# Linear attention and two expert MLPs in one launch: another loading of the values and keys, and another order of the attention's operations

## The chip, the cores and the metric

The kernel runs on one core of one Trainium2 chip. The metric is the device time of one launch, in microseconds. Of the kernel before there are three timed runs, 710.43 to 712.17 us with a median of 711.64 us, and one profiled execution.

## The reference

Three stages follow one another; all numbers are float32.

```
phi(x) = [exp(p), exp(-p)],  p = x @ w_phi - max|x @ w_phi|     q, k: (2 batches, 8 heads, 576, 64); w_phi: (64, 128)
kv = phi(k)^T @ v,  z = sum over the sequence of phi(k)
attention = (phi(q) @ kv) / (phi(q) @ z + 1e-6)                  -> x: (1152, 512)
x = (x @ w_a) * (x @ w_b) @ w_out                                w_a, w_b: (512, 1536)
out = sum over 4 experts of p_e * (relu(x @ w1[e]) @ w2[e])      w1: (4, 512, 1024); p = normalised probabilities
```

## The kernel before

**The stages.** The attention comes first, then the first MLP, then the experts, with a little overlap at the borders. The MLPs' products are made in pairs of float32r parts (a high and a low part, three matmuls for one product), and their weights are prepared ahead of their use by ScalarE, VectorE and GpSimd while TensorE multiplies.

**The attention's keys.** Keys and queries come transposed, in chunks of six tiles of 128 columns (`load_chunk`, one tile buffer `xraw` each, XB = 3 of them). Tiles are taken in groups of four; the first group of keys has two. A group of keys goes through five steps, each known by one letter: `P` projects it with w_phi into PSUM (`pj`, L185), `x` takes the maximum off (VectorE, `mx` L200 and `r` L202, once for each half of the heads), `e` makes both exponentials (ScalarE, `kp`, L211 and L212), `k` multiplies one tile's features by the values and their ones into PSUM (`kv`, L235, 8 matmuls), and after a pair of heads has all its tiles `c` and `C` copy and add it to `kvz` (ScalarE L250, VectorE L254). A tile holds 128 positions of one pair of heads, or the last 64 positions of two pairs (a tile "m").

**The queries** go through `P` and `x` too, then `r` (transposes, `rt` L267), `E` (exponentials, `qp`), and `d`, `a`, `b` (`num` L302), with a denominator and a division on ScalarE and VectorE (`D`, `n`, `X`, `Y`).

**The values.** `load_v(b, st)` (L135) loads 128 positions of all heads of batch b by two DMAs, one for the six inner heads (L142) and one for the two outer ones (L146); the last 64 positions are loaded twice, to both halves of the partitions. A batch takes 12 DMAs. Of each 192 columns the middle 64 are ones, set by GpSimd (L132).

**What sets the order.** The string SCRIPT (L34) lists the steps letter by letter, and each engine gets its instructions in that order. `v` loads a part of batch 1's values, `w` runs one task of the weights' preparation, `f` one step of the first MLP's first unit, `p` normalises the probabilities. The weights' tasks come three to a piece of weight: `begin` (ScalarE, `m` L426 and `rn` L427, reads `raw`), `middle` (VectorE L434 to L440, GpSimd L443; at its end it issues the DMAs of the piece after next, 16 for two pieces of w_a and w_b), and `parts` (ScalarE L109, GpSimd L110). There are two `raw` buffers. All these loads are issued by SP, in program order; the first two pieces are asked for by `R`.

**A chunk that is loaded twice.** At set-up `load_chunk` is called for chunks 0 to 3. When chunk 0 is used up, `stage_proj` (L191) calls `load_chunk(0 + XB)`, chunk 3 once more, into another buffer. The first copy is never read. Chunk 4 is asked for when chunk 1 is used up, and so on.

**After the attention** the function `run` (L840) steps through units of matmuls, and after each step runs `tasks_per` tasks of the weights' preparation (1.9 in the first MLP's whole units, 1.8 in its blocks). `need(u)` runs at once what is still missing of a weight.

Of the kernel before, what the change touches and what calls it, by code (L numbers as in the profile page):

```python
# [9 lines left out]
F32 = mybir.dt.float32  # L10
# [6 lines left out]
B, H, S, D = 2, 8, 576, 64  # L17
# [8 lines left out]
NTB = NT // TB  # L26
HT = S // 2
WARM = 6
XB = 3
KB = 5  # L30
RB = 11
KQ = 3
LEAD = 2
SCRIPT = "PxPeVPRxexxkekexPxevkvekkvcxkexPCkexkkevckwxCvekkwPxxkwkckCePkkwxxkekkewcePCkwxxkkePqekcxCxPekkkwxceCxwekekPxkkxkwcCkPkkkxcxCPKrxrpExEPxrxwEEEEPxdrwDxnEPErwxwxEEaPrXbEExxXdPrYwDxExwanYEXPbYxrxwPErXEEdxEDxwYraEETnXwdwffwwDbYwaXnwwfYXbwYfffXwfY"  # L34
FP1 = FA // 2
FP2 = E * FE // 2

# [17 lines left out]
def tile_linear_attention_then_mlps(ctx, tc, qT, kT, v, w_phi, wab, wout, w12, probs, out):  # L55
# [40 lines left out]

    with tc.manual_schedule():
        nc.vector.memset(zero, 0.0)
        for h in range(2):
            nc.scalar.dma_start(out=ww[D * h:D * h + D], in_=w_phi)  # L100
        warm = duo("warm", (1,))
        for k in range(WARM):
            nc.tensor.matmul(out=warm[:, 0, 0:128], lhsT=zero, rhs=zero, start=True, stop=True)
# [11 lines left out]
        def load_chunk(n):  # L115


            if n >= 2 * B * 3:
                return
            t = r_p.tile([128, NC], F32, tag="xraw", name="xraw", bufs=XB)  # L120
            src = (kT if n < B * 3 else qT)[n % (B * 3)]
            step = 256 if n == 0 else NC
            for c in range(0, NC, step):
                nc.sync.dma_start(out=t[:, c:c + step], in_=src[:, c:c + step])
            xraw[n] = t

        vt = {}
        loaded = set()

        def alloc_v(b):  # L130
            t = k_p.tile([128, 5, NP, 192], F32, tag="v", name="v", bufs=2)
            nc.gpsimd.memset(t[:, :, :, 64:128], 1.0)  # L132
            vt[b] = t

        def load_v(b, st):  # L135

            loaded.add((b, st))
            rows = v[b, st * 128:min(S, (st + 1) * 128)]
            n = rows.shape[0]
            for lo in range(0, 128, n):  # L140
                o = vt[b][lo:lo + n, st].rearrange("p a c -> p (a c)")
                nc.sync.dma_start(  # L142
                    out=o[:, 128:128 + 3 * 192].rearrange("p (a c) -> p a c", c=192)[:, :, 0:128],
                    in_=rows[:, 1:H - 1, :].rearrange("s (a h) d -> s a (h d)", h=2),
                )
                nc.sync.dma_start(  # L146
                    out=o.rearrange("p (a c) -> p a c", c=64)[:, 0:4 * NP - NP:3 * NP - 1, :],
                    in_=rows[:, 0:H:H - 1, :],
                )

        def tiles_of_batch():
# [63 lines left out]
        def stage_kv(n, k):  # L215
            kp = st_kp[n]
            assert len(kp) == 2
            kind, b, t0, t = groups[n][k]
            t = seq[t]
            if t[0] == "m":  # L220
                parts = [(t[1], 4, 0, False, True), (t[2], 4, 1, True, False)]
            else:
                p, st = t
                first, last = st == 0, st == 3
                parts = [(p, st, 0, first, last and p % 2 == 1), (p, st, 1, first and p % 2 == 0, last)]
            for p, st, half, first, last in parts:
                assert (b, st) in loaded
                if (b, p) not in kv_ps:
                    kv_ps[b, p] = duo("kv", (2, 3))
            for h in range(2):  # L230
                for s in range(2):
                    for p, st, half, first, last in parts:
                        c = 256 * h + 128 * s
                        rows = slice(64 * half, 64 * half + 64)
                        nc.tensor.matmul(  # L235
                            out=kv_ps[b, p][:, half, c:c + 128],
                            lhsT=kp[h][rows, k, s, :],
                            rhs=vt[b][rows, st, p, 64 * h:64 * h + 128],
                            start=first and h + s == 0, stop=last, skip_group_check=True,
                        )  # L240
            if t[0] == "m":
                kv_done(b, t[1])
            elif t[1] == 3 and t[0] % 2 == 1:
                kv_done(b, t[0])
# [50 lines left out]
        def stage_num(qp, kvz, k):  # L295
            t = duo("num", (2, 3) if tail[0] else range(4))
            for i in range(2):
                for s in range(2):
                    for n in range(4):
                        h = n % 2  # L300
                        c = 64 * (1 - h) if k == 0 else 64 * h + 32 * (k - 1)
                        nc.tensor.matmul(  # L302
                            out=t[32 * n:32 * n + 32, i, 0:HT],
                            lhsT=kvz[n // 2][:, h, s, c:c + 32],
                            rhs=qp[n // 2][:, s, h, HT * i:HT * i + HT],
                            start=(s == 0), stop=(s == 1), tile_position=(0, 32 * n),
                        )
            return t
# [531 lines left out]
        def run(gen, rate, tasks_per):  # L840


            for _ in gen:
                tick()
                pos[0] += 1
                credit[0] = min(credit[0] + rate, 3.0)
                while credit[0] >= 1.0 and queue and queue[0][0] <= pos[0]:
                    queue.pop(0)[2]()
                    credit[0] -= 1.0
                credit[1] = min(credit[1] + tasks_per, 2.0)  # L850
                while credit[1] >= 1.0:
                    prep(1)
                    credit[1] -= 1.0


        load_chunk(0)
        alloc_v(0)
        load_chunk(1)
        load_v(0, 0)
        load_v(0, 1)  # L860
        load_chunk(2)
        for st in range(2, 5):
            load_v(0, st)
        load_chunk(3)

        def probabilities():
            nc.vector.tensor_reduce(out=psm, in_=pr, op=ALU.add, axis=AX.X)
# [55 lines left out]
        wait["P"] = [(n,) for n in range(NG)]  # L923
        wait["r"] = [(n,) for n in range(NKG, NG)]
        wait["d"] = [(b, half) for b in range(B) for half in range(2)]
        wait["v"] = [(1, st) for st in range(5)]
        acts = {
            "P": stage_proj, "x": stage_r, "e": stage_exp, "k": stage_kv, "c": kv_copy, "C": kv_add, "r": stage_rt,
            "E": stage_eq, "d": num, "D": num_den, "n": num_rc, "a": num_part, "b": num_part, "X": product_x,
# [21 lines left out]
        order += [(FP1 - 2, 0), (FP1 - 1, 0), (FP1 - 2, 1), None, (FP1 - 1, 1)]  # L951
        for jt in order:
            if jt is None:
                run(unit_h(0, 0), 1.2, 1.6)
                continue
            j, tp = jt
            if j in BLOCKS:
                run(block_ab(j, tp), 1.0, 1.8)
                continue
            if jt == (FP1 - 2, 0):  # L960
                xc[0] = m_p.tile([128, 2, 7, 2, HT], F32R, tag="xc", name="xc")
            run(unit_ab(j, tp) if j + tp else fill, 3.0 if j == FP1 - 1 else 2.0 if jt == (FP1 - 2, 1) else 1.0, 1.9)
        xt_p.release()
        w_p.release()
        l_p = ctx.enter_context(tc.tile_pool(name="l", bufs=1, side="left", reuse_waits="tile"))
# [5 lines left out]
        for j in range(FP2):  # L971
            for tp in range(2):
                if j + tp:

                    if j == 0:
                        credit[1] = 0.0
                    run(unit_h(j, tp), 0.3 if (j, tp) == (FP2 - 1, 1) else 0.7, 1 if j else 0.7)
        drain()


# [44 lines left out]
```

## Time and profile before

| | us |
|---|---|
| median of three timed runs | 711.64 (710.43 to 712.17) |
| the profiled execution: its own time | 712.72 |
| its span, first to last instruction | 710.8 |
| TensorE busy in the span | 697.3 |
| VectorE, ScalarE, GpSimd busy | 415.7, 297.1, 275.0 |

The profiled execution took 1.08 us more than the median, and 1.92 us of it lie outside its span. A busy time counts an instruction from start to end, also where it runs slowly or overlaps the next one. PE is TensorE's matmuls, PEld its weight loads, DVE VectorE, ACT ScalarE, POOL GpSimd, SP the sync engine that issues most DMAs. A float32 matmul leaves two records, so 16 records are 8 matmuls.

### The profile page before, as it was taken

To read this page: it belongs to the slowest core of one execution; us is meant where nothing else is said; L and a number is where in the kernel's file an instruction comes from. 1 tells how busy PE (TensorE), PEld (TensorE's weight loads), DVE (VectorE), ACT (ScalarE), POOL (GpSimd) and SP (SyncE) were. 2 spreads that over 40 slices of the span, in tenths; PEclk is the share of its full clock that TensorE was granted. 3 is DMA by queue.
4 is the path that set the end of the run, shared out by engine and by line. 5 is a ranking of instruction groups with operands and counts; after the bars stand their busy time and mean duration, and the time that the engine had idled before them with its cause. 6 is when DMAs were issued, how large, how long until landed. Compare 5 with 4: busy or idle time off the path is not lost.

```text
span 710.8 us, 13103 instructions
## 1 busy us (share of the span) xinstructions
PE 697.3 (98%) x5202; PEld 641.1 (90%) x5202; DVE 415.7 (58%) x721; ACT 297.1 (42%) x595; POOL 275.0 (39%) x241
## 2 busy tenths in 40 slices
PE   8988999999999999999999999999999999999998
PEld 8986679999999999999889888988888888888887
DVE  6769956666655565545455545554545454545454
ACT  5557845455444452323642433242324242424221
POOL 1212455454443456231663434443444344434200
PEclk9999999999999999999999999999999999999999
DMA  7643123232332330012221111211021101100003
GB/s 216 172 141 98 37 85 90 60 101 82 100 80 85 90 108 13 30 60 61 60 60 59 33 58 30 60 33 57 30 60 32 58 31 60 31 31 0 1 1 134
DMA packets 49854, 46.69 MB, mean 66 GB/s; under 512 B 8320, under 2 KB 41600, under 8 KB 49792
## 3 DMA queue, kind: packets, MB, share of 16 engines
q1 hardware_dynamic: 49488, 45.65, 22.0%
q8 instruction: 41, 0.67, 0.4%
q10 hardware_dynamic: 304, 0.20, 0.1%
q14 instruction: 21, 0.17, 0.1%
HBM read 43.47 MB, written 2.36 MB: 64 GB/s over the span
## 4 chain that ended last, share of the span: by engine, by line
PE 90%; DVE 3%; ACT 2%; DMA 2%; SPq 2%; issue 1%; ACTq 0%; DVEq 0%
PE acc L817 9%; PE acc L816 9%; PE acc L815 9%; PE X L598 5%; PE X L599 5%; PE X L600 5%; PE ab L682 5%; PE ab L684 4%; PE ab L683 4%; PE num L302 3%; PE acc L713 2%; PE acc L714 2%; PE Z L598 2%; PE Z L599 2%; PE acc L712 2%; PE Z L600 2%
## 5 line engine op out<-in xcount | busy, mean ns | idle before, releaser
L825 DVE SCALAR_TENSOR_TENSOR oacc<-acc,pr,oacc 128x512 f32<-128x512 f32 (+1 forms) x136 | 101.4, 746 | 116.3 <-PE acc L817 116.3
L110 POOL TENSOR_TENSOR w<-wx,w 128x512 fp32r<-128x512 f32 x68 | 89.5, 1319 | 158.0 <-ACT w L109 153.0
L817 PE MATMUL acc<-w,hhb 128*128 128x512 f32 x290 | 114.1, 394 | 0.0
L110 POOL TENSOR_TENSOR wc<-wt,wc 128x512 fp32r<-128x512 f32 (+1 forms) x48 | 70.7, 1501 | 111.1 <-ACT wc L109 107.0
L816 PE MATMUL acc<-w,hhb 128*128 128x512 f32 x290 | 113.5, 391 | 0.0
L815 PE MATMUL acc<-w,hhb 128*128 128x512 f32 x290 | 112.9, 389 | 0.0
L443 POOL TENSOR_TENSOR wx<-wx,rn 128x512 uint32<-128x512 uint32 x36 | 47.2, 1312 | 87.2 <-DVE wx L440 87.2
L598 PE MATMUL X<-xc,wc 128*128 128x288 f32 x256 | 77.1, 301 | 0.8 <-ACT h L603 0.8
L783 ACT ACTIVATE hhb<-h 128x288 fp32r<-128x288 f32 x64 | 36.2, 566 | 99.0 <-DVE h L606 99.0
L682 PE MATMUL ab<-xh,w 128*128 128x288 f32 x256 | 75.8, 296 | 0.0
L599 PE MATMUL X<-xc,wc 128*128 128x288 f32 x256 | 75.8, 296 | 0.0
L600 PE MATMUL X<-xc,wc 128*128 128x288 f32 x256 | 75.4, 295 | 0.0
L684 PE MATMUL ab<-xh,w 128*128 128x288 f32 x256 | 75.4, 294 | 0.0
L683 PE MATMUL ab<-xl,w 128*128 128x288 f32 x256 | 75.4, 294 | 0.0
L603 ACT ACTIVATE h<-X 128x288 f32<-128x288 f32 x64 | 26.0, 407 | 107.5 <-PE X L600 107.5
L817 PEld LDWEIGHTS acc<-w,hhb 128*128 128x128 f32 x290 | 54.5, 188 | 14.1 <-DVE hhb L784 2.8
L784 DVE SCALAR_TENSOR_TENSOR hhb<-h,hhb 128x288 fp32r<-128x288 f32 x64 | 40.9, 639 | 42.8 <-ACT hhb L783 42.8
L816 PEld LDWEIGHTS acc<-w,hhb 128*128 128x128 f32 x290 | 54.4, 188 | 8.3
L815 PEld LDWEIGHTS acc<-w,hhb 128*128 128x128 f32 x290 | 54.5, 188 | 7.8
L606 DVE TENSOR_TENSOR part<-acc,part 128x288 f32<-128x288 f32 (+2 forms) x80 | 34.5, 451 | 32.7 <-PE acc L770 18.2
L109 ACT ACTIVATE w<-wx 128x512 fp32r<-128x512 f32 x68 | 42.5, 628 | 24.1 <-POOL wx L443 18.7
L598 PEld LDWEIGHTS X<-xc,wc 128*128 128x128 f32 x256 | 48.0, 188 | 4.5 <-ACT h L603 1.3
(104 smaller groups left out, 1642.5 us busy)
## 6 DMA issues: line engine op xcount, KB each, us to landing
raw<-in_wab SPq DMA_DIRECT2D x192, 64.0 KB, 2.1
wt<-in_w SPq DMA_DIRECT2D x64, 128.0 KB, 2.4
wx<-in_w SPq DMA_DIRECT2D x32, 256.0 KB, 3.0
raw<-in_wout SPq DMA_DIRECT2D x12, 512.0 KB, 3.6
xraw<-in_kT SPq DMA_DIRECT2D x6, 384.0 KB, 4.5
xraw<-in_qT SPq DMA_DIRECT2D x6, 384.0 KB, 3.1
out<-oacc SPq DMA_DIRECT2D x8, 256.0 KB, 2.0
v<-in_v SPq DMA_DIRECT2D x8, 192.0 KB, 5.1
```

The source lines that it names most:

```text
L110: eng.tensor_tensor(out=lo, in0=src, in1=hi.bitcast(F32), op=ALU.subtract)
L443: nc.gpsimd.tensor_tensor(out=x, in0=x, in1=r, op=ALU.add)
L598: nc.tensor.matmul(out=ps, lhsT=whi, rhs=xhi, start=first and a == 0, stop=False, skip_group_check=True)
L599: nc.tensor.matmul(out=ps, lhsT=whi, rhs=xlo, start=False, stop=False, skip_group_check=True)
L600: nc.tensor.matmul(out=ps, lhsT=wlo, rhs=xhi, start=False, stop=a == 1, skip_group_check=True)
L682: nc.tensor.matmul(out=t, lhsT=whi, rhs=hi, start=(c == 0), stop=False)
L683: nc.tensor.matmul(out=t, lhsT=whi, rhs=lo, start=False, stop=False)
L684: nc.tensor.matmul(out=t, lhsT=wlo, rhs=hi, start=False, stop=(c == KD - 1))
L815: nc.tensor.matmul(out=acc, lhsT=hi, rhs=whi, start=f == 0, stop=False)
L816: nc.tensor.matmul(out=acc, lhsT=hi, rhs=wlo, start=False, stop=False)
L817: nc.tensor.matmul(out=acc, lhsT=lo, rhs=whi, start=False, stop=f == 1)
L825: nc.vector.scalar_tensor_tensor(out=o, in0=acc, scalar=sc, in1=o, op0=ALU.mult, op1=ALU.add)
```

## The change

- **Values by pairs.** The 64 columns of ones now stand outside the 128 columns of a pair's two heads (13 blocks of 64 instead of 12). `load_v(b, p)` loads one pair of heads for the first 512 positions by one DMA; `load_v(b, "m")` loads the last 64 positions of all pairs by two. A batch takes 6 DMAs instead of 12, and the first pair's values are the first to be loaded. The columns that L235 and L302 read change with it.
- **Keys.** XB is 4 instead of 3, the second chunk comes in three pieces as the first does, and at set-up only chunks 0 to 3 are loaded, with chunk 4 asked for when chunk 0 is used up: each chunk is loaded once.
- **w_phi.** Its second copy is issued by GpSimd's queue instead of ScalarE's.
- **Order and sizes.** A new SCRIPT; KB (buffers of `kp`) 6 instead of 5, RB (of `r`) 8 instead of 11; other numbers of preparation tasks in a step (1.3 for 1.9, 1.6 for 1.8, 1.9 for 1.6, 0.4 for 0.7).

```diff
-XB = 3
-KB = 5
-RB = 11
+XB = 4
+KB = 6
+RB = 8
-SCRIPT = "PxPeVPRxexxkekexPxevkvekkvcxkexPCkexkkevckwxCvekkwPxxkwkckCePkkwxxkekkew...
+SCRIPT = "PPxxeRexkexekPkVkxxPkexxevkecPvkxvkkCvexewckPkxkCwevxkkckCwkkePPwewxekxk...
-        for h in range(2):
-            nc.scalar.dma_start(out=ww[D * h:D * h + D], in_=w_phi)
+        for h, eng in enumerate((nc.scalar, nc.gpsimd)):
+            eng.dma_start(out=ww[D * h:D * h + D], in_=w_phi)
-            step = 256 if n == 0 else NC
+            step = 256 if n < 2 else NC
+        VORDER = [0, "m", 1, 2, 3]
-            t = k_p.tile([128, 5, NP, 192], F32, tag="v", name="v", bufs=2)
-            nc.gpsimd.memset(t[:, :, :, 64:128], 1.0)
+            t = k_p.tile([128, 5, 64 * (3 * NP + 1)], F32, tag="v", name="v", bufs=2)
+            nc.gpsimd.memset(t.rearrange("p s (a c) -> p s a c", c=64)[:, :, 0:3 * NP + 1:3], 1.0)
-        def load_v(b, st):
-            loaded.add((b, st))
-            rows = v[b, st * 128:min(S, (st + 1) * 128)]
-            n = rows.shape[0]
-            for lo in range(0, 128, n):
-                o = vt[b][lo:lo + n, st].rearrange("p a c -> p (a c)")
+        def load_v(b, p):
+            loaded.add((b, p))
+            if p == "m":
+                for k in range(2):
+                    nc.sync.dma_start(
+                        out=vt[b][64 * k:64 * k + 64, 4, 64:].rearrange("s (a c) -> s a c", c=192)[:, k:NP:2, 0:128],
+                        in_=v[b, 512:S].rearrange("s (a h) d -> s a (h d)", h=2)[:, k:NP:2],
+                    )
+            else:
+                c = 192 * p + 64
                 nc.sync.dma_start(
-                    out=o[:, 128:128 + 3 * 192].rearrange("p (a c) -> p a c", c=192)[:, :, 0:128],
-                    in_=rows[:, 1:H - 1, :].rearrange("s (a h) d -> s a (h d)", h=2),
-                )
-                nc.sync.dma_start(
-                    out=o.rearrange("p (a c) -> p a c", c=64)[:, 0:4 * NP - NP:3 * NP - 1, :],
-                    in_=rows[:, 0:H:H - 1, :],
+                    out=vt[b][:, 0:4, c:c + 128],
+                    in_=v[b, 0:512, 2 * p:2 * p + 2, :].rearrange("(t s) h d -> s t (h d)", t=4),
                 )
-                            rhs=vt[b][rows, st, p, 64 * h:64 * h + 128],
+                            rhs=vt[b][rows, st, 192 * p + 128 * h:192 * p + 128 * h + 128],
-                        c = 64 * (1 - h) if k == 0 else 64 * h + 32 * (k - 1)
+                        c = 64 * h if k == 0 else 64 * (1 - h) + 32 * (k - 1)
         load_chunk(0)
         alloc_v(0)
+        load_v(0, 0)
         load_chunk(1)
-        load_v(0, 0)
+        load_v(0, "m")
         load_v(0, 1)
-        load_chunk(2)
-        for st in range(2, 5):
-            load_v(0, st)
-        load_chunk(3)
+        for n in range(2, XB):
+            load_chunk(n)
+            load_v(0, n)
-                run(unit_h(0, 0), 1.2, 1.6)
+                run(unit_h(0, 0), 1.2, 1.9)
-                run(block_ab(j, tp), 1.0, 1.8)
+                run(block_ab(j, tp), 1.0, 1.6)
-            run(unit_ab(j, tp) if j + tp else fill, 3.0 if j == FP1 - 1 else 2.0 if jt == (FP1 - 2, 1) else 1.0, 1.9)
+            run(unit_ab(j, tp) if j + tp else fill, 3.0 if j == FP1 - 1 else 2.0 if jt == (FP1 - 2, 1) else 1.0, 1.3)
-                    run(unit_h(j, tp), 0.3 if (j, tp) == (FP2 - 1, 1) else 0.7, 1 if j else 0.7)
+                    run(unit_h(j, tp), 0.3 if (j, tp) == (FP2 - 1, 1) else 0.7, 1 if j else 0.4)
```

The order of instructions follows from these. Line numbers behind L132 grow by one or two in the changed kernel.

SP's queue, in the kernel before, from the last chunk of keys but one to the third and fourth piece of `raw` (`raw<-in_wab`, 8 DMAs each); ahead of these rows stand the 16 DMAs of the first two pieces, a chunk, and six DMAs of batch 1's values:

```order
L124 DMA xraw<-in_kT 128x768
L142 DMA v<-in_v 128x3x128
L146 DMA v<-in_v 128x2x64
L142 DMA v<-in_v 64x3x128
L146 DMA v<-in_v 64x2x64
L142 DMA v<-in_v 64x3x128
L146 DMA v<-in_v 64x2x64
L404 DMA raw<-in_wab 32x2x256 x8
L124 DMA xraw<-in_qT 128x768
L404 DMA raw<-in_wab 32x2x256 x8
```
The same queue in the changed kernel, from chunk 4 and the 16 DMAs of the first two pieces on:

```order
L124 DMA xraw<-in_kT 128x768
L406 DMA raw<-in_wab 32x2x256 x16
L124 DMA xraw<-in_kT 128x768
L148 DMA v<-in_v 128x4x128
L124 DMA xraw<-in_qT 128x768
L142 DMA v<-in_v 64x2x128 x2
L148 DMA v<-in_v 128x4x128 x2
L406 DMA raw<-in_wab 32x2x256 x8
L148 DMA v<-in_v 128x4x128
L124 DMA xraw<-in_qT 128x768 x2
L406 DMA raw<-in_wab 32x2x256 x8
```
Between the 16 DMAs of the first two pieces and the third piece stood 14 DMAs (two chunks and all 12 of batch 1's values); now it is 7 (two chunks and five of the values).

ScalarE, in the kernel before, around the third `begin` (the rows `m` and `rn`); `kp` are exponentials of keys, `kvz` a finished pair of heads, `w` a piece of weight:

```order
L211 ACTIVATE kp<-r 128x4x128
L212 ACTIVATE kp<-r 128x4x128
L250 COPY kvz<-kv 128x512
L211 ACTIVATE kp<-r 128x4x128
L212 ACTIVATE kp<-r 128x4x128
L426 ACTIVATE m<-raw 128x512
L427 ACTIVATE rn<-raw 128x512
L211 ACTIVATE kp<-r 128x4x128
L212 ACTIVATE kp<-r 128x4x128
L211 ACTIVATE kp<-r 128x4x128
L212 ACTIVATE kp<-r 128x4x128
```
The same place in the changed kernel:

```order
L213 ACTIVATE kp<-r 128x4x128
L214 ACTIVATE kp<-r 128x4x128
L252 COPY kvz<-kv 128x512
L213 ACTIVATE kp<-r 128x4x128
L214 ACTIVATE kp<-r 128x4x128
L428 ACTIVATE m<-raw 128x512
L429 ACTIVATE rn<-raw 128x512
L252 COPY kvz<-kv 128x512
L109 ACTIVATE w<-wx 128x512
L213 ACTIVATE kp<-r 128x4x128
L214 ACTIVATE kp<-r 128x4x128
```
The third `begin` has the same place in ScalarE's order, and behind it a pair's copy and the `parts` of a piece of weight come ahead of the next exponentials.

TensorE at the start, before (`warm` are six matmuls of zeros, `pj` projections, `kv` keys by values):

```order
L103 MATMUL warm<-zero 128x128 x6
L185 MATMUL pj<-ww,xraw 128x128 x20
L235 MATMUL kv<-v,kp 128x128 x16
L185 MATMUL pj<-ww,xraw 128x128 x8
L235 MATMUL kv<-v,kp 128x128 x32
L185 MATMUL pj<-ww,xraw 128x128 x8
L235 MATMUL kv<-v,kp 128x128 x48
L185 MATMUL pj<-ww,xraw 128x128 x8
```
And in the changed kernel:

```order
L103 MATMUL warm<-zero 128x128 x6
L187 MATMUL pj<-ww,xraw 128x128 x12
L237 MATMUL kv<-v,kp 128x128 x16
L187 MATMUL pj<-ww,xraw 128x128 x8
L237 MATMUL kv<-v,kp 128x128 x16
L187 MATMUL pj<-ww,xraw 128x128 x8
L237 MATMUL kv<-v,kp 128x128 x16
L187 MATMUL pj<-ww,xraw 128x128 x8
L237 MATMUL kv<-v,kp 128x128 x32
L187 MATMUL pj<-ww,xraw 128x128 x8
```
The third group's projection (the first of the single `x8` rows) moves behind the first group's two tiles, and the fourth group's stands behind 32 matmuls of `kv` instead of 16. The fifth stands behind 48 in both.

## Rows read from the trace of the kernel before

**Rows 1.** The page's first lines: span, and each engine's busy time.
```profile
span 710.8 us, 13103 instructions
...
PE 697.3 (98%) x5202; PEld 641.1 (90%) x5202; DVE 415.7 (58%) x721; ACT 297.1 (42%) x595; POOL 275.0 (39%) x241
```

**Rows 2.** Stretches: us; busy PE, PEld, DVE, ACT, POOL; PEclk, DMA share, GB/s.
```profile
4.00:24.50 20.50, 19.73 (x326) 19.44 (x328) 16.88 (x29) 12.96 (x25) 1.27 (x1) 1.00 0.72 199
24.50:38.70 14.20, 13.51 (x238) 13.12 (x234) 9.96 (x16) 6.97 (x14) 2.55 (x2) 1.00 0.74 207
38.70:47.30 8.60, 6.36 (x64) 5.59 (x66) 4.91 (x11) 7.24 (x15) 1.27 (x1) 0.80 0.55 154
...
55.00:70.00 15.00, 11.46 (x208) 8.37 (x206) 14.12 (x28) 12.44 (x30) 3.82 (x3) 1.00 0.37 115
70.00:90.00 20.00, 19.84 (x336) 12.21 (x332) 18.87 (x33) 16.32 (x36) 9.40 (x7) 1.00 0.17 42
...
105.00:707.40 602.40, 600.45 (x3736) 560.46 (x3735) 335.54 (x581) 229.90 (x458) 244.52 (x213) 1.00 0.19 55
```

**Rows 3.** The stretch with the lower clock, cut finer (columns as above).
```profile
38.70:42.90 4.20, 1.97 (x16) 1.20 (x16) 0.73 (x2) 4.20 (x9) 0.00 (x0) 1.00 0.77 200
42.90:46.40 3.50, 3.49 (x34) 3.49 (x36) 3.40 (x8) 3.04 (x7) 1.27 (x1) 0.54 0.43 139
```

**Rows 4.** Timeline 31 to 47: start us, length us, work [idle before, releaser].
```profile
31.17 4.76 SPq L404 DMA_DIRECT2D raw<-in_wab  x8
...
38.38 0.66 ACT L426 ACTIVATE m<-raw 128x512 f32<-128x512 f32 x1 [7.23 <-DMA raw<-in_wab]
...
40.16 2.05 PE L235 MATMUL kv<-v,kp 64*128 64x128 f32 x16 [1.49 <-ACT kp L211]
...
42.17 0.69 DVE L254 TENSOR_TENSOR kvz<-kv,kvz 128x512 f32<-128x512 f32 x1 [5.16 <-ACT kvz L250]
...
42.91 3.55 PE L235 MATMUL kv<-v,kp 64*128 64x128 f32 x32 [0.71 <-DVE kvz L254]
```

**Rows 5.** Timeline of SP's queue, 11 to 31.
```profile
11.85 10.54 SPq L404 DMA_DIRECT2D raw<-in_wab  x16
...
22.43 0.42 SPq L124 DMA_DIRECT2D xraw<-in_kT  x1
...
30.44 0.62 SPq L146 DMA_DIRECT2D v<-in_v  x1
```

**Rows 6.** Timeline of TensorE's weight loads and matmuls, 15 to 26.
```profile
15.57 5.44 PEld L235 LDWEIGHTS kv<-v,kp 64*128 64x128 f32 x96
...
25.89 0.72 PE L185 MATMUL pj<-ww,xraw 64*128 64x128 f32 x8 [0.66 <-DMA xraw<-in_kT]
```

**Rows 7.** DMA issues of the whole run: KB each, median us to landing.
```profile
raw<-in_wab SPq DMA_DIRECT2D x192, 64.0 KB, 2.1
...
xraw<-in_kT SPq DMA_DIRECT2D x6, 384.0 KB, 4.5
...
v<-in_v SPq DMA_DIRECT2D x8, 192.0 KB, 5.1
...
ww<-in_w_phi ACTq DMA_DIRECT2D x2, 32.0 KB, 2.7
```

**Rows 8.** Timeline of the start: ACT's queue, TensorE, VectorE.
```profile
0.73 1.20 ACTq L100 DMA_DIRECT2D ww<-in_w_phi  x2
...
1.05 2.93 PE L103 MATMUL warm<-zero 128*128 128x128 f32 x12 [1.05 <-DVE psm L105]
...
7.29 1.16 PE L185 MATMUL pj<-ww,xraw 64*128 64x128 f32 x16 [0.77 <-PE pj L185]
...
9.75 0.68 DVE L200 TENSOR_REDUCE mx<-pj 128x4 f32<-128x512 f32 x1
```

**Rows 9.** What TensorE waited for, 105 to 711: us in total, times, longest.
```profile
PE X L598 <- ACT h L603: 0.8, 2, 0.5
```

**Rows 10.** Timeline of POOL, 270 to 400.
```profile
341.32 4.56 POOL L110 TENSOR_TENSOR wc<-wt,wc 128x768 fp32r<-128x768 f32 x3 [7.59 <-ACT wc L109]
```

More of the change, by code (lines that the diff above doesn't have):

```diff
@@ L28 @@
 WARM = 6
-XB = 3
-KB = 5
-RB = 11
+XB = 4
+KB = 6
+RB = 8
 KQ = 3
 LEAD = 2
-SCRIPT = "PxPeVPRxexxkekexPxevkvekkvcxkexPCkexkkevckwxCvekkwPxxkwkckCePkkwxxkekkewcePCkwxxkkePqekcxCxPekkkwxceCxwekekPxkkxkwcCkPkkkxcxCPKrxrpExEPxrxwEEEEPxdrwDxnEPErwxwxEEaPrXbEExxXdPrYwDxExwanYEXPbYxrxwPErXEEdxEDxwYraEETnXwdwffwwDbYwaXnwwfYXbwYfffXwfY"
+SCRIPT = "PPxxeRexkexekPkVkxxPkexxevkecPvkxvkkCvexewckPkxkCwevxkkckCwkkePPwewxekxkcCekkxxkkwcPwkkexexeqeCPxkkkPckewwkxCkkkxekPwkxkcpCxxcPCKxrPEErExxErPExxwrEEEdPxDwraxnxXPbrxwxEEEXPwrxdEYaDxEPnEXwbrYYEEPxwxXxrdExrEwDEYTnEawfwwXfdbwbawwDwwXYYwfnfffXXwfYY"
 FP1 = FA // 2
@@ L226, in stage_kv @@
             for p, st, half, first, last in parts:
-                assert (b, st) in loaded
+                assert (b, p if st < 4 else "m") in loaded
                 if (b, p) not in kv_ps:
@@ L925, in tile_linear_attention_then_mlps @@
         wait["d"] = [(b, half) for b in range(B) for half in range(2)]
-        wait["v"] = [(1, st) for st in range(5)]
+        wait["v"] = [(1, p) for p in VORDER]
         acts = {
```

## The prediction

> **What bounds the kernel now.** I read the page's first lines, then the busy times by stretch, then the waits and the timeline of the stretches in which TensorE is not full. TensorE is busy 697.3 of 710.8 us [rows 1]; a whole-run share of 98% says nothing of where the rest lies. By stretch it is this [rows 2]: from 105 to 707.4 TensorE works 600.45 of 602.40 us, so what comes before 105 only shifts that block, and it is worth little to look for time inside it. From 70 to 90 it works 19.84 of 20.00. From 55 to 70 it works 11.46 of 15.00 while VectorE works 14.12, so the queries' start is VectorE's. From 4 to 24.5 TensorE works 19.73 of 20.50. The gap is at 38.7 to 47.3: 6.36 busy of 8.60, at a granted clock of 0.80 instead of 1.00.
>
> The timeline of that gap [rows 4] shows a chain. SP issues the third piece of `raw` only at 31.17 (8 DMAs in 4.76 us). ScalarE reaches its third `begin` at 38.38 - 7.23 = 31.15 and stands until 38.38 for these data. Behind it in its queue are exponentials of keys and the copy of a finished pair; so TensorE waits 1.49 us for exponentials at 40.16, VectorE 5.16 us for the copy at 42.17, and TensorE 0.71 us more at 42.91. After that idling the clock is granted at 0.54 from 42.9 to 46.4 [rows 3], which is near the lower of its two levels (1.2 of 2.4 GHz). The rest is paid in slow matmuls: the 32 records at 42.91 take 3.55 us.
>
> The size of the loss: 96 records of `kv`, six tiles, take 5.44 us, 0.91 us a tile of 16 records [rows 6]; a projection of 16 records takes about as much (1.16 us with its drain [rows 8]). From 38.7 to 47.3 TensorE runs 64 records [rows 2], four such lots, 4 x 0.91 = 3.64 us. 8.60 - 3.64 = 4.96, so **5.0 us** are lost there.
>
> Why the third piece is late stands in SP's queue [rows 5]: 16 DMAs of pieces one and two from 11.85 to 22.4, then 14 DMAs (two chunks, twelve of values) from 22.43 to 31.06, then the third piece.
>
> **The change part by part.**
>
> *Values by pairs, keys once.* After the 16 DMAs SP has 7 to issue instead of 14. The 14 took 31.06 - 22.43 = 8.63 us, 0.62 each [rows 5], so 7 x 0.62 = 4.3 us go. Ahead of the 16 stood 19 DMAs that began at about 0.7 and ended at 11.85, 0.59 each; now there are 15 (two more for the second chunk's pieces, six fewer for the values; chunk 4 stands where chunk 3's second copy stood), 4 x 0.59 = 2.4 us. The third piece can be issued 4.3 + 2.4 = 6.7 us earlier: 31.17 - 6.7 = 24.5. With its own 4.76 us and 2.1 us to land [rows 7] it is there at 31.3, against 38.0 before. The third `begin` stands at the same place of ScalarE's order, behind equally many exponentials, copies and `begin`s, so ScalarE comes to it at about 31.2. Its wait falls from 7.23 us to about nothing. TensorE lost 5.0 us to a wait of 7.23, so some 2.2 us of such a wait are hidden by tiles whose exponentials are ready; a rest of up to 2.2 us costs nothing. Value: **-5.0**, bounds -5.0 and 0.
>
> Next late: the bytes. Up to the third piece there are 7 chunks x 384 KB, 4 x 256 + 2 x 64 KB of batch 0's values, 3 x 256 + 2 x 64 KB of batch 1's, and 3 pieces x 512 KB: 6272 KB, 6.4 MB. The trace moved 199 and 207 GB/s in the two early stretches [rows 2]: 31 to 32 us, plus the 0.7 us of the start. So the transfers themselves could hold the piece to 33, 1.8 us after ScalarE's 31.2, inside the 2.2 us. That is narrow, and a rival below.
>
> [...]
>
> *The chunk that came late.* At 25.89 TensorE waited 0.66 us for a chunk of keys [rows 6]; it is chunk 4, issued at 22.43 behind the 16 DMAs [rows 5]. It now stands ahead of them. Value **-0.7**, bounds -0.7 and 0.
>
> *The start.* The third group's projection ran at 7.29 after an idle 0.77 us, for 1.16 us, to 8.45, and VectorE took it up at 9.75, when it had done the second group [rows 8]. Now two tiles of `kv`, 2 x 0.91, stand ahead of it. If they fill the idle time from 6.5 on, it ends at 6.53 + 1.82 + 0.91 = 9.3 and VectorE loses nothing. If their exponentials come so late that they begin only where that projection ended, at 8.45, it ends at 8.45 + 1.82 + 0.91 = 11.2, 1.4 us late for VectorE. I take **+0.5**, nearer the first, because in the trace these tiles wait for nothing behind that projection, so their exponentials are there by 8.45 and may be there earlier. In the keys TensorE is nearly full, so a delay here is a delay of the end.
>
> *w_phi by two queues.* ScalarE issued both halves in 1.20 us from 0.73, and such a DMA lands in 2.7 us [rows 7, 8]: the second at 0.73 + 0.60 + 2.7 = 4.0, when the warming matmuls end (1.05 + 2.93 [rows 8]). A DMA from GpSimd is not in the trace. Issued at 0.73 like the first half it can land at 3.4, which gains nothing, since the warming matmuls stand ahead; if it lands as slowly as the values (5.1 us [rows 7], at 5.8), it costs 1.8. I take **0**, by the row of the same transfer.
>
> *Buffers and the ones.* In the new string at most five `r` are alive at once (counted letter by letter), so RB = 8 does not bind, and a sixth `kp` only loosens: 0. The wider setting of the ones is GpSimd's, which from 4 to 24.5 is busy 1.27 us [rows 2]: 0.
>
> *Fewer preparation tasks in a step.* The same tasks run, later. In before TensorE waited for no weight after 105: the longest sum in its list is 0.8 us for a copy of ScalarE's [rows 9]. Counting steps in the code, the last part of w_a and w_b's eleventh and twelfth pieces comes 3 and 2 steps ahead of its use instead of 6, and of the experts' second w1 0 instead of 2. Before, the fourth piece of w_a and w_b already stood only 1 step ahead, and no wait came of it. TensorE lacks 1.95 us of the 602.40 after 105 [rows 2], so no more than that can be won. Value 0, bounds -1.9 and +7.5 (below).
>
> *The queries' order.* The same instructions in VectorE's stretch 55 to 70; both ends taken from its TensorE idle time there, 3.54 us [rows 2]: half of it gained or lost, +-1.8. Value 0, since VectorE's 14.12 of 15.00 leave it little to gain.
>
> **Sum**: -5.0 - 0.7 + 0.5 = -5.2 us. The profiled execution took 712.72 us (710.8 span and 1.92 around it), so it would be 707.5; it stands 1.08 us above the median of the runs, so the median goes from 711.64 to **706.4**.
>
> **Rivals.**
>
> *The bytes hold the piece.* If the early transfers run at before's mean up to the third piece rather than at 200 GB/s (7 chunks, 2560 KB of values and 3 pieces are 6784 KB, 6.95 MB, in the 37.3 us to 38.0: 186 GB/s), 6.42 MB need 34.5 + 0.7 us, and ScalarE waits 4.0 us, 1.8 more than is hidden. For it: 0.72 of the DMA engines' time was already taken. Against it: SP's issuing, 0.6 us a DMA, explains before without it. -5.2 + 1.8 = -3.4: 708.2.
>
> *VectorE's stretch takes it back.* If the queries' new order makes VectorE wait as long as TensorE is now early, the change does not do what it shortens: 711.6. For it: VectorE is the bound there. Against: its work is the same, and its 5.16 us of idling at 42 goes.
>
> *Weights come late* (the slower side). One mechanism, at the weights with the short lead. `parts` of the experts' second w1 took GpSimd 341.32 to 345.88 [rows 10] with two steps in hand; a lag of the same chain by about 2.5 us at three places (eleventh and twelfth piece, second w1) is 7.5 us of waiting TensorE: -5.2 + 7.5 = +2.3: 713.9. It decides when the sum of TensorE's waits for weights after 105 passes 5 us. For it: the shorter leads. Against: the piece at lead 1 in before cost nothing.
>
> **How the numbers follow.** The forecast has 0.66, the bytes 0.13, VectorE 0.10, the weights 0.11. The likeliest alone reaches from 704.1 (no start cost, 0.5, and 1.8 of the queries' idle) to 708.5 (1.4 instead of 0.5 at the start, and 1.2 lost in the queries' order). The range that should hold 8 of 10 goes from 703.8 to 711.2: it takes in the bytes and leaves out VectorE's case, the slower one and a few hundredths below. About 0.3%, 2.1 us, is what can be told from no change: faster 0.66 + 0.11 of the bytes' = 0.77; within, 0.12; slower 0.11.
>
> **What would show it.** Right: ScalarE's wait at its third `begin` is under 2.2 us; no stretch before 55 has a granted clock below 0.9 after the start; the last keys' tiles end about 5 us earlier than before, and VectorE's full stretch begins as much earlier. Start: the third group's projection ends between 9.3 and 11.2. Wrong: a long ScalarE wait for `raw` at the third or fourth `begin`; TensorE waits behind a `w` after 105; VectorE idle over 2 us between 50 and 65.

## The result

The changed kernel takes **705.77 us**, median of six executions (705.35 to 706.11), against 711.90 (710.43 to 715.84) of the kernel before on the same chip: ratio **0.9901 (0.9874 to 0.9929)**. The forecast was 706.4. Its profiled execution has a span of 703.8 us, 7.0 less than before [rows 1]; why the span gained more than the median comes with the experiments.

The page's first lines, spans and busy times as before:

```profile
span 703.8 us, 13086 instructions
...
PE 694.3 (99%) x5202; PEld 638.3 (91%) x5202; DVE 413.2 (59%) x721; ACT 295.5 (42%) x595; POOL 274.5 (39%) x242
```

Busy time by stretch (us; busy PE, PEld, DVE, ACT, POOL; granted clock, DMA share, GB/s), the counterpart of [rows 2], with the stretch from 47.3 added and the last one cut at 700:

```profile
4.00:24.50 20.50, 19.90 (x336) 19.34 (x338) 17.27 (x29) 13.73 (x27) 2.21 (x2) 1.00 0.71 203
24.50:38.70 14.20, 14.14 (x246) 13.71 (x244) 12.62 (x23) 10.64 (x22) 4.08 (x4) 1.00 0.84 240
38.70:47.30 8.60, 8.60 (x159) 8.60 (x158) 7.63 (x15) 5.71 (x13) 2.55 (x2) 1.00 0.37 124
47.30:55.00 7.70, 5.74 (x117) 5.33 (x116) 7.49 (x14) 5.67 (x16) 0.00 (x0) 1.00 0.33 102
55.00:70.00 15.00, 14.11 (x242) 8.92 (x242) 14.41 (x27) 9.81 (x21) 3.82 (x4) 1.00 0.12 39
70.00:90.00 20.00, 19.76 (x296) 12.52 (x291) 18.12 (x29) 15.99 (x36) 12.00 (x11) 1.00 0.26 77
90.00:105.00 15.00, 15.00 (x145) 13.30 (x136) 8.71 (x14) 8.71 (x16) 9.42 (x7) 1.00 0.28 77
105.00:700.00 595.00, 593.74 (x3686) 553.73 (x3685) 326.05 (x574) 223.77 (x450) 237.52 (x209) 1.00 0.18 54
```

The gap is closed: from 38.7 to 47.3 TensorE runs 159 records, at full clock, where it ran 64. The new thin stretch is 47.3 to 55, the queries' start, where VectorE is the full engine (7.49 of 7.70). This stretch began about 55 before.

The clock from 42.9 to 46.4, 0.54 in [rows 3], is 1.00:

```profile
42.90:46.40 3.50, 3.50 (x68) 3.50 (x66) 3.36 (x7) 1.70 (x4) 1.27 (x1) 1.00 0.34 133
```

The timeline around the third `begin` (start us, length us, work, in brackets idle before and its releaser), the counterpart of [rows 4]:

```profile
27.01 4.84 SPq L406 DMA_DIRECT2D raw<-in_wab  x8
...
33.90 1.96 PE L237 MATMUL kv<-v,kp 64*128 64x128 f32 x32
...
33.95 0.67 ACT L428 ACTIVATE m<-raw 128x512 f32<-128x512 f32 x1 [2.80 <-DMA raw<-in_wab]
...
36.14 3.57 PE L237 MATMUL kv<-v,kp 64*128 64x128 f32 x48
...
40.43 5.53 PE L237 MATMUL kv<-v,kp 64*128 64x128 f32 x96
```

ScalarE still waits 2.80 us for the third piece, but TensorE has tiles all the while: it is busy 14.14 of 14.20 us and 8.60 of 8.60 us in the two stretches around the wait. The last keys: the first transposes of queries (`rt`), which follow the last keys' projection, began at 54.9 and now begin at 48.9; the first MLP's first product with `hhb` began at 112.6 and now begins at 106.0. So 6.0 of the 7.0 us are there when the queries' transposes begin, 6.6 at that product. Before and after, by tile and by line (duration ns least, median, most, then first and last start):

```profile
L267 PE MATMUL rt<-ident,r x144: 216/222/273, 54.9 to 85.8; 64*128 64x64 f32 x144
...
L712 PE MATMUL acc<-hhb,w x128: 288/294/397, 112.6 to 334.7; 128*128 128x288 f32 x128
```
```profile
L269 PE MATMUL rt<-ident,r x144: 216/223/274, 48.9 to 79.2; 64*128 64x64 f32 x144
...
L714 PE MATMUL acc<-hhb,w x128: 288/295/399, 106.0 to 327.6; 128*128 128x288 f32 x128
```

### The profile page after: what moved, and what is told of

Read it like the earlier page. It is cut to its first block, busy times and chain, and to the rows that moved or that the text cites. A ratio compares the mean times of both kernels' runs of the same rounds, so it can differ in the third digit from the quotient of the medians.

```text
span 703.8 us, 13086 instructions
## 1 busy us (share of the span) xinstructions
PE 694.3 (99%) x5202; PEld 638.3 (91%) x5202; DVE 413.2 (59%) x721; ACT 295.5 (42%) x595; POOL 274.5 (39%) x242
## 4 chain that ended last, share of the span: by engine, by line
PE 92%; DVE 5%; issue 1%; ACT 0%; POOL 0%; SPq 0%; DVEq 0%; ACTq 0%
PE acc L819 10%; PE acc L818 9%; PE acc L817 9%; PE X L600 5%; PE X L601 5%; PE X L602 5%; PE kv L237 5%; PE ab L685 4%; PE ab L684 4%; PE ab L686 4%; PE acc L715 2%; PE Z L600 2%; PE acc L716 2%; PE Z L601 2%; PE acc L714 2%; PE Z L602 2%
## 5 line engine op out<-in xcount | busy, mean ns | idle before, releaser
L445 POOL TENSOR_TENSOR wx<-wx,rn 128x512 uint32<-128x512 uint32 x36 | 46.4, 1289 | 95.9 <-DVE wx L442 95.9
L600 PEld LDWEIGHTS X<-xc,wc 128*128 128x128 f32 x256 | 48.0, 188 | 4.3 <-ACT h L605 0.7
L601 PEld LDWEIGHTS X<-xc,wc 128*128 128x128 f32 x256 | 48.2, 188 | 2.7
```

The costliest lines, as they stand in the source:

```text
L445: nc.gpsimd.tensor_tensor(out=x, in0=x, in1=r, op=ALU.add)
L600: nc.tensor.matmul(out=ps, lhsT=whi, rhs=xhi, start=first and a == 0, stop=False, skip_group_check=True)
L601: nc.tensor.matmul(out=ps, lhsT=whi, rhs=xlo, start=False, stop=False, skip_group_check=True)
```

## The experiments

Ratios are to the kernel before on the same chip, with 95% intervals. Beside the time stands the start of the first transposes of queries, a marker that the trace gives to 0.1 us (54.9 before, 48.9 and 49.2 in two traces of the changed kernel). The executions of the kernel before fall into two groups by their granted clock, described at *Chunk 3 once*. The ratios mix the two groups; the gains against its executions at full clock alone stand there too.

**The loads alone.** All of the change's loads and XB (RB stays at 8, for room), with the old order, KB, numbers of tasks and w_phi.

The edit of the changed kernel, beside w_phi and the numbers:

```diff
-KB = 6
-SCRIPT = "PPxxeRexkexekPkVkxxPkexxevkecPvkxvkkCvex...
+KB = 5
+SCRIPT = "PxPeVPRxexxkekexPxevkvekkvcxkexPCkexkkev...
```

> The kernel before with the new loads alone (values by pairs, ones outside, XB = 4, second chunk in pieces, each chunk once, RB = 8 for room); SCRIPT, KB, preparation rates and w_phi as before. Theory (ScalarE's wait for the third piece of raw is the loss, and SP's shorter list takes it away): that wait falls from 7.2 to under 3 us, the clock stays at 1.00 in 38 to 47, and the time falls by 4.5 to 6 us. Rival (the new order brings the gain): it falls by less than 1.5 us.

708.29 us, 0.9945 (0.9925 to 0.9965); marker 49.9. ScalarE's wait is shorter but not gone, and from 38.7 to 47.3 TensorE is not quite full:

```profile
34.97 0.67 ACT L428 ACTIVATE m<-raw 128x512 f32<-128x512 f32 x1 [4.62 <-DMA raw<-in_wab]
...
38.70:47.30 8.60, 7.90 (x142) 7.78 (x140) 8.22 (x16) 6.30 (x14) 2.54 (x2) 1.00 0.48 150
```

So the loads carry 5.0 of the 6.0 us at the marker without the new order. The mechanism is the theory's, but both of its sizes are missed: the wait is 4.62 us and not under 3, the time falls by 4.1 us and not by 4.5 to 6.

**The order alone.** The kernel before with the new SCRIPT, KB and RB.

```diff
-KB = 5
-RB = 11
-SCRIPT = "PxPeVPRxexxkekexPxevkvekkvcxkexPCkexkkev...
+KB = 6
+RB = 8
+SCRIPT = "PPxxeRexkexekPkVkxxPkexxevkecPvkxvkkCvex...
```

> The kernel before with the new SCRIPT, KB = 6 and RB = 8 alone; all loads and the preparation rates as before. Theory: the third piece still comes at about 38, ScalarE waits 6 us or more for it, TensorE idles behind, and the time changes by less than 1.5 us. Rival (the new order brings the gain): it falls by 4 us or more.

716.00 us, 1.0051 (1.0032 to 1.0069), slower; marker 56.6. The new order with the old loads still meets a late piece, and TensorE waits behind it for longer:

```profile
37.42 0.66 ACT L426 ACTIVATE m<-raw 128x512 f32<-128x512 f32 x1 [4.42 <-DMA raw<-in_wab]
...
38.69 2.46 PE L235 MATMUL kv<-v,kp 64*128 64x128 f32 x15 [3.80 <-ACT rn L427]
```

It also waits for values three times, 2.5 us in all. Theory and rival are both missed: ScalarE's wait was to be 6 us or more and the time to change by less than 1.5 us, or to fall by 4. The order is no gain by itself; what it adds to the new loads comes below.

**w_phi alone.**

```diff
-        for h in range(2):
-            nc.scalar.dma_start(out=ww[D * h:D * h + D], in_=w_phi)
+        for h, eng in enumerate((nc.scalar, nc.gpsimd)):
+            eng.dma_start(out=ww[D * h:D * h + D], in_=w_phi)
```

> The kernel before with the second copy of w_phi issued by GpSimd, nothing else. After the result the traces show the first 24 projection records in 1.73 us instead of 2.60, and VectorE's first maximum at 4.80 instead of 5.51. Theory now: the second copy of w_phi was what they waited for, so the first maximum comes 0.6 to 0.8 us earlier and the time falls by 0.4 to 0.8 us. Rival (the first projections were slow by TensorE's start, or a DMA from GpSimd lands no earlier): the first maximum stays at 5.5 and the time within 0.3 us.

712.59 us, 1.0003 (0.9985 to 1.0021); marker 54.9. There is no difference that this interval, 1.3 us to either side, can tell, and the theory's 0.4 to 0.8 us lie inside it. The first maximum is at 5.19 in this trace, 0.3 us earlier than in the trace of before, and the marker does not move.

**One letter.** The kernel before, with the `w` that issues the third `begin` moved 18 letters later, to just before the `w` of the next `parts`. No load is touched.

```diff
-...ewcePCkwxxkkePqekcxCxPekkkwxceCxwek...
+...ewcePCkxxkkePqekcxCxPekkkwwxceCxwek...
```

> The kernel before with one letter of SCRIPT moved: the third begin stands three pairs of exponentials and a copy later, directly ahead of its piece's next use of the slot, loads and all else as before. Theory (the loss comes of what is queued behind the waiting begin on ScalarE): the third piece lands at 38 as before, but ScalarE waits under 2 us, TensorE keeps its clock, and the time falls by 3.5 to 5 us with no load changed. Rival (the keys or values themselves are late, or the DMA engines are the bound): within 1 us of before.

707.36 us, 0.9936 (0.9913 to 0.9960), 5.0 us less than before; marker 49.2. SP issues the piece as late as before, and nothing waits for it:

```profile
31.03 5.11 SPq L404 DMA_DIRECT2D raw<-in_wab  x8
...
37.96 0.68 ACT L426 ACTIVATE m<-raw 128x512 f32<-128x512 f32 x1 [0.20 <-issue]
...
38.70:47.30 8.60, 8.60 (x160) 8.60 (x158) 7.31 (x15) 5.59 (x12) 2.56 (x2) 1.00 0.82 230
```

This is the test that settles the mechanism: the time was lost because ScalarE stood in its own order at a wait, not because TensorE needed the piece by then. The piece comes as late as before, and TensorE is full.

**The values alone.** The six DMAs of a batch instead of twelve and the ones outside; chunk 3 still loaded twice, XB still 3.

```diff
-        def load_v(b, st):
+        def load_v(b, p):
```

> The kernel before with the values loaded by pairs and their ones outside, nothing else: chunk 3 is still loaded twice, XB = 3, old order and rates. SP has 13 DMAs ahead of the first 16 of raw (19 before) and 8 between those and the third piece (14 before). Theory (the values' 12 DMAs a batch made the third piece late): the third begin runs at 34 to 36 instead of 38.4, TensorE loses under 2 us in 38 to 47 instead of 5, the time falls by 2.5 to 4.5 us. Rival (the second copy of chunk 3 or XB made it): it falls by less than 1 us.

709.21 us, 0.9945 (0.9925 to 0.9966); marker 51.2, wait at the third `begin` 4.54. The theory holds in the medians: the time falls by 4.0 us, TensorE is busy 8.10 of 8.60 us from 38.7 to 47.3; only the `begin`, at 36.27, is a little later than expected.

**Chunk 3 once.** The kernel before, without the first load of chunk 3.

```diff
-        load_chunk(3)
```

> The kernel before without the first, never read load of chunk 3, nothing else. Theory: one DMA of 384 KB less ahead of the first pieces of raw; the third piece comes 0.6 to 1.5 us earlier, ScalarE still waits over 5 us for it, the time falls by 0.3 to 1.5 us. Rival (this load made the third piece late): it falls by over 2.5 us.

709.60 us, 0.9962 (0.9944 to 0.9980), 3.6 us under its partner's 713.19, where its own trace shows only a marker of 54.1 (-0.8) and a span of 710.4 (-0.4). The clock explains half of this. That trace still holds the stall, at a low clock (stretch as in [rows 3]), and ScalarE's wait is 6.54 us, as expected:

```profile
42.90:46.40 3.50, 3.50 (x40) 3.50 (x40) 3.37 (x8) 2.26 (x6) 1.26 (x1) 0.57 0.37 107
```

Its 11 executions fall in two groups: seven at a mean granted clock of 0.999 or 1.000 take 708.5 to 710.3, four at 0.998 take 711.6 to 712.7. The kernel before does the same: of 53 executions beside these experiments 25 show 1.000 (median 710.96) and 28 show 0.994 to 0.998 (median 713.57). The changed kernel's eleven (two sets) all show 0.999 or 1.000 and spread 0.9 us. In all five traces at 0.994 to 0.998 (before, the order alone, w_phi alone, this one, the new numbers alone) the fall lies in this stretch, 38.7 to 47.3 (0.80, 0.80, 0.80, 0.80, 0.63). So the stall costs 2.6 us more in those executions in which the clock falls in it, about half of them. The deeper fall goes with the longer time: of the 28, the 14 at 0.998 have a median of 712.45, the 14 at 0.994 or 0.995 one of 713.82. No execution of before at full clock was traced, so its stall is known by its time alone. Measured from the 1.000 group the change gains 5.2 us, from the other 7.8. The profile of before [rows 1] is of the lower clock, hence the 7.0 of its span, and the medians before wander (711.5 to 713.2) by how many executions fall in each group.

Group against group, chunk 3 loaded once gains 1.8 us in either (709.36 against 711.16, 712.20 against 713.95); the other half of the 3.6 us is that fewer of its executions show the fall (four of eleven, against ten of sixteen). 1.8 us is more than the expected 0.3 to 1.5, and its trace places only 0.8 of it, at the marker. Against the executions of before at full clock in its set, the loads alone bring 2.4 us (708.29 against 710.70), one letter 3.3 (707.36 against 710.70) and the values alone 2.1 (709.07 at full clock, against 711.16). The order alone, with the lower clock in all eight executions, loses 2.9 us to before's executions of the lower clock (716.00 against 713.05).

**The old numbers of tasks in the changed kernel.**

```diff
-                run(unit_h(0, 0), 1.2, 1.9)
+                run(unit_h(0, 0), 1.2, 1.6)
-                run(block_ab(j, tp), 1.0, 1.6)
+                run(block_ab(j, tp), 1.0, 1.8)
-...2.0 if jt == (FP1 - 2, 1) else 1.0, 1.3)
+...2.0 if jt == (FP1 - 2, 1) else 1.0, 1.9)
-...0.7, 1 if j else 0.4)
+...0.7, 1 if j else 0.7)
```

> The changed kernel with the four old numbers of preparation tasks in a step (1.6, 1.8, 1.9, 0.7). Theory (nothing after 105 waits for weights in either): within 0.5 us of the changed kernel, 705.8 to 706.5. Rival (the rates are worth the 0.7 us that TensorE's idle time after 105 fell by): 0.6 to 1.0 us slower than the changed kernel.

708.17 us, 0.9932 (0.9912 to 0.9951), 2.3 us more than the changed kernel with `p` late in the same set (below). That is more than the theory (within 0.5) and the rival (0.6 to 1.0) allowed. The marker is 48.7 and the first product with `hhb` at 105.8, so nothing of it is in the attention.

**`p` last.** The changed kernel with the probabilities' letter moved from place 122 to the string's end (the first rows of the edit show where it is taken out).

```diff
-...xekPwkxkcpCxxcPCKxr...
+...xekPwkxkcCxxcPCKxr...
```

> The changed kernel with one letter of SCRIPT moved: p, the normalisation of the probabilities, four small VectorE instructions that took 1.77 us at 44.10, comes last in SCRIPT. VectorE is full from 43 to 66 while TensorE idles 1.96 us in 47.3 to 55. Theory (VectorE's stretch sets when the TensorE-bound part begins): the time falls by 0.7 to 1.8 us, to 704.0 to 705.1. Rival (the stretch has slack): within 0.4 us.

705.90 us, 0.9899 (0.9879 to 0.9918): the changed kernel's time. The theory falls; the stretch has slack for these four instructions.

**The new numbers in the kernel before.** The four numbers the other way round.

```diff
-...2.0 if jt == (FP1 - 2, 1) else 1.0, 1.9)
+...2.0 if jt == (FP1 - 2, 1) else 1.0, 1.3)
```

> The kernel before with the four new numbers of preparation tasks in a step, nothing else. Theory A (the numbers matter only behind the new order, where the tasks left over from the keys and queries collide with the products' copies): within 0.5 us of the kernel before, ratio 0.9993 to 1.0007, and from the first product with w_a and w_b to the first X 188.0 to 188.6 us against 188.4. Rival B (the old numbers cost the same 2.3 us with any order): about 710, ratio 0.997.

712.86 us, 1.0016 (1.0003 to 1.0029): rival B falls. Eleven of its 12 executions are of the lower clock (median 712.91; in this set the kernel before has 712.19 there, in 5 of 17), one is at 1.000 (711.06, against 711.05). From the first product with `hhb` to the first X it takes 188.9 us, 0.3 more than theory A allowed. In the kernel before the new numbers bring nothing, and TensorE waits once, 0.7 us, for a part of a weight (`w`, GpSimd) between 105 and 300.

**Loads and letter.** The loads alone, with the moved letter as well; and this with the new numbers.

```diff
-...ewcePCkwxxkkePqekcxCxPekkkwxceCxwek...
+...ewcePCkxxkkePqekcxCxPekkkwwxceCxwek...
```

> The kernel before with the new loads (values by pairs, keys once), the old order and old numbers, and in that order the third `begin` moved to just before the first `parts` behind it, as in the run that moved it alone. Theory A (two causes of one wait: taking it away by either recovers the same 5 us, and the loads add only chunk 4's 0.7): 706.5, ratio 0.992, ScalarE's third `begin` without a wait. Rival B (the gains of 4.1 and 5.0 add): 703.3, ratio 0.987.

With the new numbers:

> The same with the new numbers of preparation tasks as well; what is left of the change is its order of the keys and queries, and w_phi. Theory A: 706 to 706.5, so that the changed kernel's order of operations is worth no more than 0.5 us beyond one moved `begin`. Rival B (the order has a gain of its own in the keys and at the start): over 707, 1 us or more slower than the changed kernel of this job.

The changed kernel itself beside them:

> The changed kernel again, as the measure for the other three on the same chip: 705.8, ratio 0.990.

706.65 us, 0.9933 (0.9917 to 0.9949), and 706.87, 0.9934 (0.9919 to 0.9949), beside the changed kernel's 705.91, 0.9918 (0.9903 to 0.9934). Theory A holds for the first: its third `begin` has no wait, and the two ways to take the wait away do not add. By the marker the loads alone bring 5.0 us, the letter alone 5.7, both 6.4 (48.5); against before's executions at full clock 2.4, 3.3 and 4.4. For the second it is missed: with the new numbers the time stays 1.0 us above the changed kernel, where 0.5 was the limit, so what is left of the change (its order, KB and w_phi) has a small gain of its own, near the rival's. Where it lies is shown in part: there the marker is 49.3 and the first product with `hhb` at 107.0 (49.2 and 106.2 in the changed kernel's trace of this set), and TensorE waits 0.7 us for a part of a weight at 129.40. What the changed kernel has beyond the first, 0.7 us, is not in the keys. It is here (with the old order, ScalarE and TensorE at 164 to 167):

```profile
164.86 0.66 ACT L428 ACTIVATE m<-raw 128x512 f32<-128x512 f32 x1 [3.95 <-DMA raw<-in_wab]
...
165.97 0.67 ACT L605 ACTIVATE hhb<-gg 128x576 fp32r<-128x576 f32 x1
...
166.69 0.40 PE L714 MATMUL acc<-hhb,w 128*128 128x288 f32 x1 [1.68 <-ACT hhb L605]
```

and in the changed kernel:

```profile
163.13 0.67 ACT L428 ACTIVATE m<-raw 128x512 f32<-128x512 f32 x1 [3.54 <-DMA raw<-in_wab]
...
164.26 0.67 ACT L605 ACTIVATE hhb<-gg 128x576 fp32r<-128x576 f32 x1
...
165.77 0.40 PE L715 MATMUL acc<-hhb,w 128*128 128x288 f32 x1 [0.39 <-DVE hhb L697]
```

It is the attention's stall once more: a `begin` that waits for `raw` with a copy behind it that TensorE needs. In the changed kernel the piece is there 1.7 us earlier and the copy is in time. The changed kernel with the old numbers has the `begin` at 165.00 and a wait of 0.99 us at 166.84; from 105 to 300 its TensorE is busy 192.90 of 195 us instead of 194.41. Why the piece comes later there was not pursued.

None of these runs beats the changed kernel.

## Why the prediction was right

**The stall (-5.0): right in its mechanism, and shown; two of its terms are mis-sized.** One moved letter gives 5.0 us in the medians, the new loads alone 4.1. The first mis-sized term is the time at which the piece is there. It was not 31.3, as the sum from SP's issuing had it, but 33.9, where the bytes' estimate of 33 stood nearer. SP was to begin the piece 6.7 us earlier; in this trace it began 4.2 us earlier, at 27.01 instead of 31.17. The 7 DMAs taken out behind the 16 did count, 3.7 us for an estimated 4.3. The four fewer ahead of them were to bring 2.4 us and brought 0.5: the 16 began 3.0 us earlier, at 8.88 instead of 11.85, but took 13.00 instead of 10.54:

```profile
8.88 13.00 SPq L406 DMA_DIRECT2D raw<-in_wab  x16
21.99 0.37 SPq L124 DMA_DIRECT2D xraw<-in_kT  x1
...
24.66 2.24 SPq L148 DMA_DIRECT2D v<-in_v  x2
27.01 4.84 SPq L406 DMA_DIRECT2D raw<-in_wab  x8
```

Over the runs they end between 20.6 and 23.0 wherever they begin (8.7 to 14.6): started at 12.82 with the values alone they take 9.27, at 14.62 with the order alone 8.34.

An earlier start of the piece itself did not help either. In the second trace of the changed kernel SP begins it at 25.15, 6.0 us earlier than before, and the `begin` runs no earlier:

```profile
25.15 5.60 SPq L406 DMA_DIRECT2D raw<-in_wab  x8
...
34.21 0.67 ACT L428 ACTIVATE m<-raw 128x512 f32<-128x512 f32 x1 [2.68 <-DMA raw<-in_wab]
```

In the four traces with the new loads and the new order (the changed kernel twice, the old numbers, `p` last) SP begins the piece between 24.69 and 27.01 and the `begin` stands between 33.71 and 34.25, and the latest start, 27.01, has the second earliest `begin`, 33.95. So the time of arrival does not follow from the time of issue. That the transfers hold the piece fits this, but no run shows it.

The second mis-sized term is the margin. The -5.0 was read from an execution in which the clock fell, and holds that loss: from 42.9 to 46.4 TensorE ran 34 records, where the changed kernel runs 68, so about 1.7 us of the 5.0 (an estimate) are slow matmuls, and 3.3 are what the wait itself cost. By this estimate 3.9 of the 7.23 us were hidden and not 2.2. It agrees with the letter's 3.3 us against before's executions at full clock, and with the waits of 4.62 and 4.54 us of the loads alone and the values alone, which left TensorE short of 0.70 and 0.50 us from 38.7 to 47.3. The sign that was named, a wait under 2.2 us, did not come: it was 2.80, and it cost TensorE nothing. The rival of the bytes, which had ScalarE wait 4.0 us, was 1.2 us off in the wait; with 3.9 us hidden it would have cost next to nothing.

**Chunk 4 (-0.7): right.** TensorE works 14.14 of 14.20 us from 24.5 to 38.7 (13.51 before), and no wait for a chunk is left in its list. Chunk 3 loaded once gives 0.8 at the marker.

**The start (+0.5): right for the place, but not felt.** The third group's projection ends at 9.56, in the forecast's 9.3 to 11.2:

```profile
4.80 0.42 DVE L202 TENSOR_REDUCE mx<-pj 128x2 f32<-128x256 f32 x1 [3.77 <-PE pj L187]
...
8.50 1.06 PE L187 MATMUL pj<-ww,xraw 64*128 64x128 f32 x16
...
9.61 0.69 DVE L202 TENSOR_REDUCE mx<-pj 128x4 f32<-128x512 f32 x1 [0.49 <-PE pj L187]
```

VectorE takes it up 4.81 us after its first maximum; before it was 4.24 (9.75 less 5.51), which is the 0.57 that the estimate gave. The first maximum came 0.7 us earlier, which hides it. In the second trace of the changed kernel the first maximum is at 5.17 and the third group is taken up at 9.98, 0.2 us later than before. Over the runs the first maximum comes between 4.80 and 5.61, and at 6.23 with the values alone, where TensorE waited 0.27 us for w_phi at 4.97. Apart from that it follows no edit, and why it varies is open.

**w_phi (0): right** as far as the interval tells, 1.0003 (0.9985 to 1.0021). The Trainium skill (Trainium Kernel Development and Optimization, Key Constraints) says that the DMAs of the SP, ScalarE and GpSimd queues run on the same 16 DMA engines, and that issuing from several engines at once saves the issue time alone. This run, the one in which nothing but the spreading of a load over two queues was changed, agrees.

**Fewer tasks in a step (0, bounds -1.9 and +7.5): wrong in its reason.** The text took the numbers as a risk to the weights, with nothing to win, since the list of waits after 105 was short in the trace before. In the kernel before they indeed bring nothing. But in the changed kernel the old numbers cost 2.3 us. 1.5 of them are in the stretch from 105 to 300, where TensorE waits 1.3 us for ScalarE's copies `hhb` (0.2 in the changed kernel) and 0.8 for VectorE's (0.4); the longest, 0.99, is for a copy queued behind a `begin` that waits for its piece. A list of waits shows what the kernel's present timing brings out; an earlier front brings out others. The list of the changed kernel from 105 on (us in total, times, longest) has no wait for a weight:

```profile
PE X L600 <- ACT h L605: 0.5, 1, 0.5
PE acc L715 <- DVE hhb L697: 0.4, 1, 0.4
PE X L600 <- DVE h L608: 0.2, 1, 0.2
PE acc L714 <- ACT hhb L605: 0.2, 1, 0.2
```

So the rival of late weights did not come about, at the shorter leads that were counted. It is not empty: with the old order and the new numbers (two traces) TensorE waited 0.7 us once for a part of a weight.

**The queries (0 +-1.8): the stretch did not take the gain back.** The 6.0 us at the queries' first transposes have become 6.6 at the first product with `hhb`. VectorE is idle 0.8 us in all of 47.3 to 70. `p`, which the new order puts at the end of the keys, makes no difference to the time.

**The sum.** It was -5.2 against the profiled execution of before, so 707.5; the changed kernel's profiled one took 705.69, 1.8 less. 0.8 of this is in the keys (6.0 for 5.2; the moved letter alone brings 5.7 there, where the stall was put at 5.0), 0.6 between there and 106, 0.4 behind. The 1.08 us taken off for the median offset part of it. They were not a mere offset, since the profiled execution was one with the clock's fall in it; against the executions of before at full clock the change brings 5.2, which the sum meets only by chance.

## What to carry over

A wait that an engine takes in its order costs what stands behind it: look there before speeding up the transfer, since moving the waiting instruction by a few places may recover as much as fewer DMAs do (here 3.3 and 2.4 us against the executions of before at full clock, and 4.4 together). Keep a loss by waiting apart from one by the clock that falls behind it, or the hidden part of the wait comes out too small (here 2.2 us for an estimated 3.9). Do not take the time at which data are there from the time of issue alone: count a DMA taken out ahead of a long burst as a gain only where the burst ends earlier; here its end stayed within 2.4 us while its start moved by 5.9. Where executions of a kernel spread by more than those of its neighbours, look for a stall in which the clock falls in some of them, and compare executions of like clock.

## What the runs showed of the hardware

**VectorE beside GpSimd.** A small VectorE instruction took six times its usual time beside one of GpSimd. `p`'s second step, on 128 x 9 elements, took 0.17 us before at 56.92; in the changed kernel (timeline):

```profile
44.09 1.27 POOL L110 TENSOR_TENSOR w<-wx,w 128x512 fp32r<-128x512 f32 x1 [2.92 <-ACT w L109]
44.10 0.18 DVE L869 TENSOR_REDUCE psm<-pr 128x9 f32<-128x36 f32 x1
...
44.32 1.07 DVE L870 TENSOR_SCALAR psm<-psm 128x9 f32<-128x9 f32 x1
```

It ends at 45.39, and GpSimd's instruction at 45.36. In two more traces the step starts at another point of GpSimd's instruction and again ends with it: 0.75 us, to 45.32, beside one that ends at 45.29 (the changed kernel again), and 0.65 us, to 44.82, beside one that ends at 44.80 (the old numbers). In before and with `p` last, where GpSimd does nothing at the time, it takes 0.17. The reduction that ran beside the same instruction took 0.18, as without one. The Trainium skill (SBUF — State Buffer, "SBUF: two separate sides") says that some VectorE instructions and GpSimd's take a shared pair of ports whole, so that the one that starts second waits for the end of the first; the rows agree.
